# Attention with top-k and a channel mix: small products moved to GpSimd, weights split another way, weighings joined, mix chunks placed one by one

## The chip, the core and the metric

The kernel runs on one core of a Trainium2 chip. The metric is the device time of one execution in microseconds (us). Five engines work on their own queues, in the order of the program: TensorE (PE, with its weight loads shown apart as PEld), VectorE (DVE), ScalarE (ACT), GpSimd (POOL) and the queue that issues most transfers (SP).

## The reference

```python
scores = scale * q @ k.T                      # 8 batches, 8 heads, 576 x 576
kth = the 32nd largest score of each row
scores = where(scores >= kth, scores, -1e9)
attn = exp(scores - max); attn /= attn.sum(-1) + 1e-09
x = (attn @ v), heads side by side            # 8 x 576 x 512
xk = mu_k * x + (1 - mu_k) * x_prev           # x_prev: x one row earlier
xr = mu_r * x + (1 - mu_r) * x_prev
k = relu(xk @ w_k); v = (k * k) @ w_v         # 512 -> 1024 -> 512
out = sigmoid(xr @ w_r) * v
```

q, k and v are float32; w_k, w_v and w_r lie in memory as float64, 4 MB each for w_k and w_v and 2 MB for w_r.

## The kernel before, in words

**Attention.** Heads go in pairs; one pair of one batch has 1152 rows of scores, cut into 9 tiles of 128 rows, and the 288 tiles of the whole input come in 64 visits (tiles 0 to 3 of a pair, then 4 to 8). For a tile, TensorE makes the scores (`score`, `sliver`, or `score8` for the ninth tile, L824, L825, L833, L837), ScalarE copies them into `sc` (L842), and VectorE finds the 24 largest of a row: seven maxima of pieces (`cand`, L847), then three maxima with two removals between them (`best`, `drop`, L849, L852). `under` (L859) multiplies the largest and the 24th by two constants in one VectorE instruction of two columns; the results are the biases of `exps` and `count`. ScalarE's `count` (L867) marks what lies below the 24th, GpSimd's `below` (L869) multiplies scores and marks, VectorE takes the next eight (`eighth`, L870) and picks the threshold (`nine`, L872). ScalarE makes the exponentials (L875), VectorE masks and sums them (`mask`, L878), TensorE transposes them (`turn`, L883, and `turnl`, L892), ScalarE copies the transposes out, and TensorE multiplies by v (`weigh`, L912 and L913), one group of ten products for each two tiles. For up to four tiles the sums get 1e-9 (`inv`, L923) and a reciprocal (`inv2`, L924) on VectorE, are spread on GpSimd (L930), transposed (L934), copied out, and `place` (L947, L949) writes the rows of x into `xT`.

**Mix.** 18 chunks of 256 rows. GpSimd and ScalarE form xk and xr and split each into two parts in a reduced float32 (`change`, `share`, `add`, `xh`, `xl`); TensorE then multiplies in three products each (L620 to L622): 96 `hidden`, 24 `gate` and 48 `value` matmuls a chunk; ScalarE and GpSimd square and split what lies between (`relu`, `sq`, `r2`, `hl`), VectorE multiplies gate and value (`gated`, L1076).

**Weights.** 20 blocks of 128x512 float64 numbers are loaded as 32-bit words and turned into two float32 parts by bit work. Eight blocks of w_k go through four staging slots that later hold `hh` and `hl`; the twelve blocks of w_r and w_v go through two slots that lie in the `xT` buffer of the second batch, so `place` of that batch waits for the last of them. A block takes ScalarE `wabs` (L1118), VectorE `wclamp`, `wshift`, `wsign`, `wexp` (L1119 to L1122), ScalarE `wfine`, `whi` (L1126, L1127, for w_v `whalf` too), GpSimd `wmul` (L1128). The lower part is made for the first twelve blocks by three TensorE matmuls (`wsub`, L1134) and a ScalarE copy (L1136), for the last eight by a subtraction and an addition on GpSimd (L1138, L1139).

**What sets the order.** The program builds a graph of these steps and a planner lists them: each step has an engine, a cost, a latency and a key (its tile number plus an offset from the tables `OFF`, `HEAD`, `TAIL`), and of the steps of an engine that can start about first the one with the smallest key goes next. The mix is a single chain of pieces on TensorE, held back by `pace`, and the start of chunk c was worked out from the tiles that it needs (L997 to L999). The order of each queue is thus fixed before the run.

Of the kernel before, what the change touches and what calls it, by code (L numbers as in the profile page):

```python
# [20 lines left out]
TOPK = 32  # L21
# [24 lines left out]
BACK = False
HOLD = 0
PAIR = False
WCL = 0
# [4 lines left out]
def visits():  # L54

    vs = []
    for b in range(B):
        for k, part in enumerate(EDGE.get(b, HALVES)):
            for hp in range(HP)[::-1] if BACK and k % 2 else range(HP):
                if vs and vs[-1][:2] == (b, hp):  # L60
                    part = range(vs.pop()[2][0], part[-1] + 1)
                vs.append((b, hp, part))
                part = EDGE.get(b, HALVES)[k]
    return vs
# [1240 lines left out]
```

## Time and profile before

| what | value |
|---|---|
| median of 3 runs | 1198.69 us (1198.59 to 1199.99) |
| the profiled execution | 1199.56 us, its span 1197.8 us |
| granted TensorE clock, mean | 0.983 of full speed |
| instructions | 27941 |

The profile shows the span of one execution; what lies around it is 1.8 us here. In the rows below a busy share is the time in which an engine had an instruction at work, and a waiting time is put down to what ended it.

### The profile page before, as it was taken

Reading aid. Unit: us, or ns where it says so; the run is one execution under the profiler, and the core shown is the slowest. Engines: PE = TensorE matmul, PEld = TensorE weight load, DVE = VectorE, ACT = ScalarE, POOL = GpSimd, SP = SyncE. Lnnn points to the kernel's source line nnn. Section 1 sums busy time; section 2 is a strip of 40 time slices with the busy share of each in tenths; the row PEclk is TensorE's granted clock in tenths of the full one; section 3 lists DMA queues with packets and bytes.
Section 4 is the critical chain, followed back from the end, with each engine's and each line's share of the span. In section 5 each row is a group of like instructions: output and inputs, shape, how many; then the busy total and the mean of one; then the engine's idle time right before and its main releaser. Section 6 shows DMA issues by size and latency. Waiting matters only on the chain.

```text
span 1197.8 us, 27941 instructions
## 1 busy us (share of the span) xinstructions
PE 1145.7 (96%) x8717; PEld 877.5 (73%) x8717; DVE 1100.1 (92%) x6180; ACT 1030.9 (86%) x2205; POOL 865.8 (72%) x796
## 2 busy tenths in 40 slices
PE   5887799999999999999999999999999999999998
PEld 2444576878787877777777878787878787878886
DVE  6999999999999999999999999999999999999500
ACT  5898898999899999999899899989888989888631
POOL 2557896868686877778687677868686867777763
PEclk9887899999999999999999999999999999999999
DMA  6132212212122112221221212121221121211000
GB/s 241 50 130 86 83 46 76 63 55 69 53 79 67 54 54 76 63 81 43 77 64 54 69 54 69 54 72 54 67 68 58 56 68 56 68 48 37 18 19 21
DMA packets 36012, 78.43 MB, mean 65 GB/s; under 512 B 4112, under 2 KB 12304, under 8 KB 35856
## 3 DMA queue, kind: packets, MB, share of 16 engines
q1 hardware_dynamic: 35568, 76.17, 20.2%
q8 instruction: 71, 1.16, 0.4%
q14 instruction: 85, 0.70, 0.2%
q10 hardware_dynamic: 288, 0.39, 0.1%
HBM read 67.11 MB, written 9.44 MB: 64 GB/s over the span
## 4 chain that ended last, share of the span: by engine, by line
PE 48%; DVE 42%; ACT 6%; issue 2%; DMA 1%; POOL 0%; SPq 0%; DVEq 0%; ACTq 0%
DVE cand L847 11%; PE rot L620 8%; PE rot L622 8%; PE rot L621 8%; DVE E L878 8%; DVE top L870 7%; PE ps L912 6%; PE rot L883 6%; PE ps L837 5%; DVE top L849 4%; DVE cand L852 4%; DVE nine L872 2%; PE ps L824 1%; PE ps L913 1%; ACT sc L842 1%
## 5 line engine op out<-in xcount | busy, mean ns | idle before, releaser
L869 POOL TENSOR_TENSOR sg<-sc,sg 128x576 f32<-128x576 f32 x288 | 410.1, 1425 | 220.4 <-ACT sg L867 218.8
L847 DVE MAX8 cand<-sc 128x8 f32<-128x82 f32 (+1 forms) x2016 | 387.8, 231 | 5.5 <-ACT sc L842 4.6
L867 ACT ACTIVATE sg<-sc,seen 128x576 f32<-128x576 f32 x288 | 223.6, 777 | 24.8 <-DVE seen L859 23.6
L878 DVE SCALAR_TENSOR_TENSOR E<-sc,seen,se 128x576 f32<-128x576 f32 x288 | 230.4, 800 | 0.4 <-ACT se L875 0.2
L875 ACT ACTIVATE se<-sc,seen 128x576 f32<-128x576 f32 x288 | 215.5, 748 | 17.6 <-DVE E L878 12.4
L842 ACT ACTIVATE sc<-ps 128x576 f32<-128x576 f32 x288 | 184.9, 650 | 42.5 <-PE ps L837 15.6
L870 DVE MAX8 top<-sg 128x8 f32<-128x576 f32 x288 | 215.0, 747 | 4.1 <-POOL sg L869 3.9
L883 PE MATMUL rot<-ident,E 128*128 128x128 f32 x1152 | 179.7, 280 | 10.1 <-ACT ri L939 2.6
L883 PEld LDWEIGHTS rot<-ident,E 128*128 128x128 f32 x1152 | 131.5, 142 | 71.9 <-issue 11.1
L849 DVE MAX8 top<-cand 128x8 f32<-128x56 f32 x864 | 176.7, 207 | 1.6
L885 ACT ACTIVATE et<-rot 128x512 f32<-128x512 f32 x288 | 171.5, 598 | 3.7 <-PE rot L883 2.6
L620 PE MATMUL rot<-xh,wk 128*128 128x256 f32 x576 | 171.8, 298 | 0.3 <-ACT ri L940 0.2
L912 PE MATMUL ps<-et,v 128*64 128x128 f32 (+1 forms) x2560 | 166.8, 272 | 3.7 <-DVE xT L947 1.7
L912 PEld LDWEIGHTS ps<-et,v 128*64 128x64 f32 x2560 | 130.2, 139 | 53.3 <-issue 17.2
L621 PE MATMUL rot<-xl,wk 128*128 128x256 f32 x576 | 161.9, 281 | 0.5 <-POOL xl L1033 0.5
L622 PE MATMUL rot<-xh,wk 128*128 128x256 f32 x576 | 162.0, 281 | 0.0
L837 PE MATMUL ps<-K,qs 64*128 64x512 f32 x512 | 151.9, 671 | 0.0
L620 PE MATMUL rot<-wv,hh 128*128 128x512 f32 x288 | 123.7, 430 | 0.6 <-DVE eb L1076 0.6
L620 PEld LDWEIGHTS rot<-xh,wk 128*128 128x128 f32 x576 | 109.4, 190 | 9.0 <-issue 5.7
L852 DVE MATCH_REPLACE8 cand<-top,cand 128x56 f32<-128x56 f32 x576 | 115.5, 200 | 0.2 <-issue 0.2
L622 PE MATMUL rot<-wv,hl 128*128 128x512 f32 x288 | 113.7, 395 | 0.0
L621 PE MATMUL rot<-wv,hh 128*128 128x512 f32 x288 | 113.6, 394 | 0.0
(95 smaller groups left out, 2361.0 us busy)
## 6 DMA issues: line engine op xcount, KB each, us to landing
v<-in_v SPq DMA_DIRECT2D x64, 384.0 KB, 3.1
K<-in_k SPq DMA_DIRECT2D x64, 320.0 KB, 3.0
out<-eb SPq DMA_DIRECT2D x35, 256.0 KB, 2.0
qs<-in_q SPq DMA_DIRECT2D x32, 192.0 KB, 2.4
stage<-in_moe_w_k SPq DMA_DIRECT2D x8, 512.0 KB, 5.1
xT<-in_moe_w_v SPq DMA_DIRECT2D x8, 512.0 KB, 3.6
qs<-in_q SPq DMA_DIRECT2D x31, 128.0 KB, 2.1
xT<-in_moe_w_r SPq DMA_DIRECT2D x4, 512.0 KB, 6.1
```

Source lines behind the costliest of these rows:

```text
L620: return [nc.tensor.matmul(ps, lhsT=sh, rhs=mh, start=first, stop=False), nc.tensor.matmul(ps, lhsT=sh, rhs=ml, start=False, stop=False), ...
L621: nc.tensor.matmul(ps, lhsT=sh, rhs=ml, start=False, stop=False),
L622: nc.tensor.matmul(ps, lhsT=sl, rhs=mh, start=False, stop=last)]
L847: lambda T=T, c=c: nc.vector.max(T.cand.t[:, 8 * c:8 * c + 8], T.sc.t[:, CUTS[c]:CUTS[c + 1]]), reads=[T.sc], writes=[(T.cand, c)])
L849: plan.op(DVE, "best", n + BESTS * r, 120, 217, lambda T=T, r=r: nc.vector.max(T.top.t[:, r * 8:(r + 1) * 8], T.cand.t), reads=[T.cand], w ...
L867: lambda T=T, sn=sn: nc.scalar.activation(T.side.t, T.sc.t, AF.Sign, bias=sn(T, 1), scale=-BELOW, accum_out=T.top.t[:, TOPK:TOPK + 1]),
L869: plan.op(POOL, "below", n, 1375, 1430, lambda T=T: nc.gpsimd.tensor_mul(T.side.t, T.sc.t, T.side.t), reads=[T.sc], writes=[T.side])
L870: plan.op(DVE, "eighth", n, 660, 754, lambda T=T: nc.vector.max(T.top.t[:, 24:32], T.side.t), reads=[T.side], writes=[(T.top, 3)])
L875: plan.op(ACT, "exps", n, 667, 754, lambda T=T, pe=pe, sn=sn: nc.scalar.activation(pe.t, T.sc.t, AF.Exp, bias=sn(T, 0), scale=SCALE), read ...
L878: lambda T=T, U=U, pe=pe, sn=sn: nc.vector.scalar_tensor_tensor(T.e(), T.sc.t, sn(T, 2), pe.t, op0=OP.is_ge, op1=OP.mult, accum_out=U.rs.t ...
L883: return [nc.tensor.transpose(pt.t[:, c * 128:(c + 1) * 128], E.t[:, o + c * 128:o + (c + 1) * 128], ident) for c in range(NKC)]
L912: return [*[nc.tensor.matmul(pa[hs[j]], lhsT=vs[j][:, c, :], rhs=ms[c][j], start=(c == 0), stop=False) for c in range(NKC) for j in range(2)],
```

## The change

- `under` goes from VectorE to GpSimd, with its two constants in an SBUF tile `factors` instead of PSUM; `inv` too.
- The weight blocks are split another way. A block is loaded twice, the second time one 16-bit word further on (`wm`). ScalarE takes a scaled copy of the high words into PSUM (`wabs`) and their signs (`wsign`), VectorE shifts (`wshift`) and masks (`wrest`) with one side in PSUM, GpSimd multiplies in the sign (`wput`) and the exponent (`wmul`). `wclamp`, `wsub` on TensorE and the subtraction and addition on GpSimd are gone.
- The two weighings of a unit of four tiles are one step on TensorE, listed once both have their inputs.
- `score8` has one product with the last 64 keys instead of two; the tile of K is 704 columns wide instead of 640.
- The start of each mix chunk is a number of its own (`AT`); all tables of offsets have other numbers, there is a third table for the first 24 tiles (`FIRST`), and buffers differ: `et` 5 (was 3), `el` 3 (2), `sg` 3 (2), `eb` 3 (4), `K` 2 (3), no `lb`.

```diff
-MORE = dict(xh=2, xl=2, et=3, top=3, el=2, K=3, eb=4, lb=2)
+MORE = dict(xh=2, xl=2, et=5, top=3, el=3, eb=3, sg=3, K=2)
...
+AT = [-6.03, -8.616, 62.223, 51.725, 69.632, 81.783, 97.48, 87.342, 134.245, 89.408, 140.491, 139.103, 174.089, 182.425, 241.323, 261.83, 194.143, 348.355]
...
                         return [nc.tensor.matmul(ps[0].t, lhsT=qd, rhs=P.K.t[:, :MAIN], start=True, stop=True),
-                                *[nc.tensor.matmul(sl.t[:, MAIN:S], lhsT=qd, rhs=P.K.t[:, MAIN + h * REST:MAIN + (h + 1) * REST], start=h == 0, stop=h == 1) for h in range(2)]]
+                                nc.tensor.matmul(sl.t[:, MAIN:S], lhsT=qd, rhs=P.K.t[:, MAIN:S], start=True, stop=True)]
...
-                    plan.op(DVE, "under", n, 62, 160, lambda T=T, hp=hp: nc.vector.tensor_mul(T.seen.t[:, hp, 0:2, T.i], T.top.t[:, 0:24:23], X.ranks.t[:, 9:11]),
+                plan.op(POOL, "under", n, 140, 200, lambda T=T, hp=hp: nc.gpsimd.tensor_mul(T.seen.t[:, hp, 0:2, T.i], T.top.t[:, 0:24:23], factors),
...
-                    if not PAIR or u == (U.w - 1) // 2:
+                    if u == (U.w - 1) // 2:
                         fs, cs, rs, ws = zip(*U.weigh)
-                        U.weigh = []
                         plan.op(PE_, "weigh", n, sum(cs), sum(cs) + 197, lambda fs=fs: [x for f in fs for x in f()], reads=[x for r in rs for x in r] + [P.v], writes=ws, mode="W")
...
-                    plan.op(DVE, "inv", n, 60, 155, lambda w=w, U=U, pr=pr: nc.vector.tensor_scalar(pr.t[:, :w], U.rs.t[:, :w], 1e-9, None, op0=OP.add), reads=[U.rs], writes=[pr])
+                    plan.op(POOL, "inv", n, 120, 180, lambda w=w, U=U: nc.gpsimd.tensor_scalar(U.rs.t[:, :w], U.rs.t[:, :w], 1e-9, 1.0, op0=OP.add, op1=OP.mult), writes=[U.rs], mode="TS")
...
-            r = max(ready[b, u] for b, s, m in pieces for u in units_of(b, s, m)) + min(LAG, LAG0 + c * LAG1)
-            at = max(at, r)
-            key = lambda x, at=at, n=n: at + x * STEP * n / CH / 20
+            key = lambda x, at=AT[c], n=n: at + x * STEP * n / CH / 20
...
-            plan.op(DVE, "wclamp", key, 588, 692, lambda: nc.vector.tensor_scalar(pm.t, pm.t, ZERO, None, op0=OP.max), writes=[pm])
-            plan.op(DVE, "wshift", key, 588, 692, lambda: nc.vector.tensor_scalar(U(pm), U(pm), 3, 0x3FFFFFFF, op0=OP.logical_shift_left, op1=OP.bitwise_and), writes=[pm])
-        plan.op(DVE, "wsign", key, 588, 692, lambda: nc.vector.scalar_tensor_tensor(U(val), high(), 0xC0000000, U(pm), op0=OP.bitwise_and, op1=OP.bitwise_or), reads=[st, pm], writes=[val])
...
-            X.subs.append(plan.op(PE_, "wsub", key, 2050, 2250, rest, reads=[val, fine, (W, ('h', which))], writes=[pl], mode="T"))
-            done.append(plan.op(ACT, "wlo", key, 520, 630, lambda: nc.scalar.activation(lo, pl.t, AF.Copy), reads=[pl], writes=[(W, which)]))
...
+        plan.op(SP, "w", key, 600, 4500, lambda: nc.sync.dma_start(st.t.bitcast(U16), words), writes=[st])
+        plan.op(ACT, "wabs", key, 552, 640, lambda: nc.scalar.activation(pm.t, high().bitcast(F32), AF.Copy, scale=TINIER), reads=[st], writes=[pm])
+        plan.op(DVE, "wshift", key, 595, 695, lambda: nc.vector.tensor_scalar(bits(), pm.t.bitcast(U32), 3, 0x7FFFF000, op0=OP.logical_shift_left, op1=OP.bitwise_and), reads=[pm], writes=[val])
+        plan.op(ACT, "wsign", key, 552, 640, lambda: nc.scalar.activation(flat(), high().bitcast(F32), AF.Sign), reads=[st], writes=[mag])
...
+            plan.op(POOL, "wput", key, 1400, 1440, lambda: nc.gpsimd.tensor_mul(hi, val.t, flat()), reads=[val, mag], writes=[(W, ('h', which))])
+            plan.op(DVE, "wexp", key, 650, 750, lambda: nc.vector.tensor_scalar(flat().bitcast(U32), hi.bitcast(U32), 0xFF800000, None, op0=OP.bitwise_and), reads=[(W, ('h', which))], writes=[mag])
+        plan.op(SP, "wm", key, 600, 4500, lambda: nc.sync.dma_start(sm.t.bitcast(U16)[:, :2046], words[:, 1:2047]), writes=[sm])
+        plan.op(DVE, "wrest", key, 595, 695, lambda: nc.vector.tensor_scalar(pr.t.bitcast(U32), sm.t.rearrange("p (c t) -> p c t", t=2)[:, :, 0], 0x1FFFFFF, None, op0=OP.bitwise_and), reads=[sm], writes=[pr])
+        plan.op(ACT, "wfine", key, 560, 667, lambda: nc.scalar.activation(fine(), pr.t.bitcast(U32), AF.Copy, scale=2.0 ** (-37 if name == "v" else -36)), reads=[pr], writes=[sm])
+        done.append(plan.op(POOL, "wmul", key, 1400, 1440, lambda: nc.gpsimd.tensor_mul(lo, fine(), flat()), reads=[mag, sm], writes=[(W, which)]))
```

The order of the queues, at three places. First TensorE in the first third of the program, at the weighing of two tiles of one unit (et: transposed tiles, el: their last columns, ps: scores and sums, K and qs: the operands of a score). Before:

```order
L912 MATMUL ps<-et_112,v_84 64x128
L913 MATMUL ps<-el_115,v_84 64x128 x2
L837 MATMUL ps<-K_87,qs_88 128x512 x2
L620 MATMUL rot_143<-xh_121,wk_66 128x256
L621 MATMUL rot_143<-xl_123,wk_66 128x256
```

and in the changed program:

```order
L912 MATMUL ps<-et_114,v_87 64x128
L912 MATMUL ps<-et_115,v_87 64x128
L913 MATMUL ps<-el_120,v_87 64x128 x2
L912 MATMUL ps<-et_116,v_87 64x128
L912 MATMUL ps<-et_117,v_87 64x128
```

Before, a weighing of two tiles is followed by other work; now the weighing of the next two tiles stands directly behind it. Over the program the groups of weighings go from 160 to 96, the places where TensorE leaves a score or a weighing of half the array for something else from 288 to 224, and those where it enters one from whole-array work from 195 to 178.

Second, VectorE at the first weight blocks (stage and xT: staged words, rot: PSUM, eb, r: block-sized buffers). Before:

```order
L1119 TENSOR_SCALAR rot_141<-rot_141 128x512
L849 MAX top_96<-cand_94 128x8
L1119 TENSOR_SCALAR rot_142<-rot_142 128x512
L852 MATCH_REPLACE cand_94<-top_96,cand_94 128x56
L1120 TENSOR_SCALAR rot_141<-rot_141 128x512
L1120 TENSOR_SCALAR rot_142<-rot_142 128x512
L849 MAX top_96<-cand_94 128x8
L1121 SCALAR_TENSOR_TENSOR eb_127<-stage,rot_141 128x512
L859 TENSOR_TENSOR seen_103<-top_96,se 128x2
L1121 SCALAR_TENSOR_TENSOR eb_128<-stage,rot_142 128x512
```

and in the changed program:

```order
L1120 TENSOR_SCALAR rot_143<-xT_137 128x512
L858 MATCH_REPLACE cand_96<-top_98,cand_96 128x56
L1110 TENSOR_SCALAR eb_133<-rot_142 128x512
L855 MAX top_98<-cand_96 128x8
L1120 TENSOR_SCALAR rot_142<-stage 128x512
L858 MATCH_REPLACE cand_96<-top_98,cand_96 128x56
L1110 TENSOR_SCALAR eb_134<-rot_144 128x512
L855 MAX top_98<-cand_96 128x8
L1110 TENSOR_SCALAR eb_135<-rot_143 128x512
L1120 TENSOR_SCALAR rot_144<-stage 128x512
L1118 TENSOR_SCALAR r_131<-wr_70 128x512
```

A block has three VectorE instructions instead of four, and the product `seen<-top` has left the queue. In the old order all 80 weight instructions of VectorE stand ahead of the 28th mask; in the new one 54 of 60 stand ahead of the 30th, and the last ahead of the 37th. The first hidden product of the mix stands on TensorE behind 19 turned tiles before and behind 20 now.

Third, GpSimd in the middle of the program (sg: marked scores, hl, xl, xm: parts of the mix, seen: the two products). Before:

```order
L869 TENSOR_TENSOR sg_99<-sc_90,sg_99 128x576
L1033 TENSOR_TENSOR xl_123<-xm_120,xh_121 128x512
L1033 TENSOR_TENSOR xl_123<-xm_119,xh_121 128x512
L869 TENSOR_TENSOR sg_100<-sc_91,sg_100 128x576
L930 TENSOR_SCALAR ri_116<-rs_108 128x128
```

and in the changed program:

```order
L1026 TENSOR_TENSOR xl_129<-xm_126,xh_127 128x512
L1026 TENSOR_TENSOR xl_129<-xm_125,xh_127 128x512
L864 TENSOR_TENSOR seen_106<-top_100,factors 128x2
L869 TENSOR_TENSOR sg_102<-sc_92,sg_102 128x576
L1045 TENSOR_TENSOR r_132<-r_132 128x512
L864 TENSOR_TENSOR seen_106<-top_98,factors 128x2
L869 TENSOR_TENSOR sg_103<-sc_93,sg_103 128x576
```

The small product of a tile now stands in the queue of GpSimd's long products, about one tile ahead of the `below` of its own tile.

## Rows read from the trace of the kernel before

**Rows 1.** The page's first part: busy us, share of the span, instructions.

```profile
PE 1145.7 (96%) x8717; PEld 877.5 (73%) x8717; DVE 1100.1 (92%) x6180; ACT 1030.9 (86%) x2205; POOL 865.8 (72%) x796
```

**Rows 2.** Stretches: length, busy us of PE, PEld, DVE, ACT, POOL, clock, DMA share, GB/s.

```profile
8.20:160.00 151.80, 115.06 (x653) 70.09 (x654) 147.19 (x677) 128.95 (x262) 99.13 (x83) 0.88 0.32 105
160.00:1120.00 960.00, 955.98 (x7617) 744.57 (x7618) 944.74 (x5482) 874.81 (x1893) 725.42 (x670) 1.00 0.20 61
1120.00:1190.00 70.00, 70.00 (x439) 60.67 (x436) 6.83 (x18) 25.13 (x50) 40.40 (x36) 1.00 0.06 20
```

**Rows 3.** One stretch, TensorE alone.

```profile
160.00:1190.00 1030.00, 1025.98 (x8052) 1.00 0.19 58
```

**Rows 4.** One line of each: operation, count, ns min/median/max, first and last start.

```profile
L1119 DVE TENSOR_SCALAR rot<-rot x20: 669/683/699, 10.6 to 152.4; 128x512 f32<-128x512 f32 x20
L859 DVE TENSOR_TENSOR seen<-top,se x288: 130/143/163, 14.7 to 1118.1; 128x2 f32<-128x2 f32 x144
L620 PE MATMUL rot<-xh,wk x576: 277/281/581, 116.9 to 1174.6; 128*128 128x256 f32 x192
```

**Rows 5.** Timeline of VectorE, 12.8 to 14.8 us: start, us, line.

```profile
12.81 1.28 DVE L1120 TENSOR_SCALAR rot<-rot 128x512 uint32<-128x512 uint32 x2
...
14.72 0.15 DVE L859 TENSOR_TENSOR seen<-top,se 128x2 f32<-128x2 f32 x1
14.78 0.68 DVE L1121 SCALAR_TENSOR_TENSOR eb<-stage,rot 128x512 uint32<-128x512 uint32 x1
```

**Rows 6.** Stretches, the instructions of L859 alone.

```profile
0.00:160.00 160.00, 4.21 (x29) 0.88 0.34 113
```

**Rows 7.** Timeline of TensorE, 805 to 814 us.

```profile
805.63 0.60 PE L883 MATMUL rot<-ident,E 128*128 128x128 f32 x4
806.16 1.09 PE L912 MATMUL ps<-et,v 128*64 128x128 f32 x16
807.08 0.39 PE L913 MATMUL ps<-el,v 128*64 128x128 f32 x4
807.40 1.13 PE L837 MATMUL ps<-K,qs 64*128 64x512 f32 x4
...
812.11 0.60 PE L883 MATMUL rot<-ident,E 128*128 128x128 f32 x4
812.54 1.02 PE L824 MATMUL ps<-K,qs 128*128 128x512 f32 x2
813.40 0.56 PE L825 MATMUL ps<-K,qs 128*128 128x64 f32 x4
813.80 0.28 PE L892 MATMUL ps<-ident,E 128*128 128x128 f32 x1
```

**Rows 8.** Groups of GpSimd instructions by form: busy us, mean ns, idle before.

```profile
L1128 POOL TENSOR_TENSOR lb<-lb,r 128x512 f32<-128x512 f32 x20 | 25.7, 1285 | 12.4 <-ACT lb L1126 9.9 <-DVE r L1122 2.5
L1029 POOL TENSOR_TENSOR xm<-xm,xT 128x256 f32<-128x256 f32 x16 | 10.7, 690 | 1.1 <-ACT xm L1024 1.0
L1029 POOL TENSOR_TENSOR xm<-xm,xT 128x128 f32<-128x128 f32 x16 | 7.1, 446 | 0.2 <-ACT xm L1024 0.2
```

**Rows 9.** Waits of GpSimd: who waited for whom, us, times, longest.

```profile
POOL sg L869 <- ACT sg L867: 218.8, 154, 15.0
```

**Rows 10.** Loads of weight blocks: KB each, median us to landing.

```profile
xT<-in_moe_w_v SPq DMA_DIRECT2D x8, 512.0 KB, 3.6
xT<-in_moe_w_r SPq DMA_DIRECT2D x4, 512.0 KB, 6.1
```

**Rows 11.** Stretches, TensorE's `wsub` (L1134) alone: busy PE, busy PEld.

```profile
0.00:160.00 160.00, 28.43 (x60) 11.38 (x60) 0.88 0.34 113
```

**Rows 12.** Stretches of all engines, columns as in rows 2.

```profile
0.00:20.00 20.00, 10.48 (x21) 4.15 (x22) 10.55 (x41) 9.54 (x16) 4.44 (x12) 1.00 0.89 334
...
130.00:140.00 10.00, 6.09 (x37) 3.61 (x36) 9.00 (x32) 7.26 (x14) 9.27 (x9) 0.66 0.15 43
140.00:150.00 10.00, 9.41 (x78) 7.54 (x77) 9.07 (x50) 8.27 (x20) 7.57 (x7) 1.00 0.18 68
```

More of the change, by code (lines that the diff above doesn't have):

```diff
@@ L57, in visits @@
     for b in range(B):
[L58 to L61, printed above, removed]
+        for part in EDGE.get(b, HALVES):
+            for hp in range(HP):
                 vs.append((b, hp, part))
-                part = EDGE.get(b, HALVES)[k]
     return vs
@@ L89 @@
-TAIL = dict(addr=9.764, wshift=-54.034, wexp=12.766, sq=46.852, lowt=0.774, sliver=-0.915, whi=18.971, xlk=10.89, xhk=11.972, store=21.562,
-            nine=-22.73, best=11.307, wclamp=-30.249, lowr=15.632, hl=-29.505, turni=-0.007, xhr=-12.539, relu=-3.644, kt=-26.88, drop=1.635,
-            gate=23.895, score8=-15.705, eighth=4.543, under=5.446, inv2=-16.489, v=18.41, w=-5.629, wmul=11.119, wfine=-13.156, lowest=23.573,
-            gexp=-39.54, score=-0.308, sharek=16.794, wabs=-18.436, exps=3.896, nmu=-26.956, below=0.218, changek=-0.251, lowc=14.381, wsub=8.41,
-            inv=-21.671, low=9.578, gated=-2.041, turnl=3.662, place=0.456, ri=-33.859, r2=4.155, weigh=1.655, spread=-7.304, kq=12.986, cand=16.257,
-            value=25.102, hidden=7.542, zero=-6.282, ranks=-14.357, mu=-14.658, count=20.929, mask=-6.883, wsign=1.775, xlr=17.098, wlo=-3.664,
-            keep=-1.091, addk=2.852, el=-2.717, sharer=-17.211, turn=1.382, et=4.439, whalf=5.878)
+NEAR = dict(PE=142.316, ACT=94.901, DVE=1.447, POOL=234.747, SP=6.125)
@@ new lines @@
+HEAD = dict(sharek=-47.371, zero=154.778, lowt=-23.559, score8=-11.785, store=209.645, el=-79.186, gate=-26.338, turni=91.426, sq=26.461, hl=113.15,
+            relu=-47.049, wmul=-27.583, low=-6.219, xhk=61.499, inv=110.857, v=-12.116, gated=-131.363, xlk=16.829, turn=42.663, r2=4.269,
+            xlr=16.635, addr=-200.707, ri=-66.902, below=-14.314, best=-24.605, wabs=-59.334, lowr=180.774, sliver=-116.326, nmu=14.466, kq=141.279,
+            changek=39.743, count=-13.892, hidden=6.777, addk=-98.359, xhr=95.257, lowc=60.575, eighth=-56.451, w=172.797, kt=1.172, wshift=-10.774,
+            wexp=15.565, ranks=119.206, spread=32.638, mask=-44.708, whi=179.551, drop=-62.419, gexp=65.164, keep=-94.404, inv2=-20.263, mu=-116.499,
+            weigh=-64.727, turnl=48.3, score=-5.275, under=-90.964, nine=-79.706, place=-5.27, sharer=50.724, et=33.131, wfine=30.879,
+            wsign=-118.488, exps=-49.391, lowest=-68.808, value=60.46, cand=6.626, wrest=5.672, wm=2.948, wput=-29.083)
@@ new lines @@
+TAIL = dict(addr=75.077, wshift=-71.426, wexp=88.368, sq=220.928, lowt=-151.351, sliver=-126.01, whi=-14.333, xlk=100.276, xhk=54.542, store=-72.657,
+            nine=53.016, best=55.339, lowr=9.427, hl=81.731, turni=-109.29, xhr=45.326, relu=-18.048, kt=30.108, drop=85.184, gate=-36.159,
+            score8=-63.376, eighth=-43.894, under=-43.046, inv2=-36.699, v=29.142, w=-96.933, wmul=0.662, wfine=26.729, lowest=-64.048, gexp=123.791,
+            score=-32.419, sharek=-17.199, wabs=-168.587, exps=2.264, nmu=-196.418, below=26.843, changek=-82.372, lowc=17.854, inv=270.105,
+            low=-26.01, gated=77.754, turnl=33.065, place=59.611, ri=124.319, r2=-54.949, weigh=-98.505, spread=-120.091, kq=-22.273, cand=60.211,
+            value=5.334, hidden=-50.412, zero=35.483, ranks=-27.964, mu=85.532, count=39.835, mask=101.415, wsign=37.272, xlr=118.137, keep=-40.713,
+            addk=3.005, el=-27.772, sharer=-104.183, turn=-6.619, et=-42.42, wrest=30.561, wm=-111.8, wput=-71.442)
@@ L776, in attend @@
         buf = plan.buf
[L777 to L778 removed]
+        xT = {}
+        seen = None
         for p, (b, hp, part) in enumerate(visits):
```

184 lines of the change are left out of this document (76 added, 108 removed).

## The prediction

> **What bounds the kernel now.** I read the busy times first, then cut the span into stretches, then asked which engine never rests in each. Over the span TensorE is busy 96% and VectorE 92% [rows 1], which names no single bound. The stretches do [rows 2]. From 8.2 to 160 us VectorE is busy 147.2 of 151.8 us, while TensorE has 36.7 us without work: this is the **head**, in which the weights are converted beside the first 29 tiles. From 160 to 1190 us TensorE is busy 1026 of 1030 us [rows 3]: there nothing but TensorE's own work sets the time. VectorE is nearly full too until 1120 us [rows 2], but it is done 70 us before TensorE, so it follows there. The end is therefore the length of the head plus the TensorE work that is left behind it. GpSimd, with 725 of 960 us in the long stretch, has 235 us of room.
>
> **The head.** VectorE decides, so I count what leaves and joins its queue up to the 29th tile. Before, all 80 weight instructions lie there; after, 54 of 60 do, the rest behind: 26 fewer. One takes 0.684 us by its record [rows 4], but two in a row take 1.28 us together, so the next starts after 0.59 us [rows 5]. 26 x 0.59 = 15.3 us (by records, 17.8). That the new shift reads PSUM and writes SBUF, and the new mask the other way round, has no row; both lie between forms with one or two PSUM sides that take 0.67 to 0.69 us [rows 4, 5], so I take them as equal. The 29 `under` products have 4.2 us of records there [rows 6]; the next instruction starts 0.06 us behind one [rows 5], so they give back 1.7 to 4.2 us, taken as 2. `inv`, nine times here, is as small: below 1 us, taken as 0.5. Against it stands one tile more ahead of the first hidden product (20 instead of 19): VectorE's share of a tile here is (147.2 - 80 x 0.59)/29 = 3.4 us, but the tile's TensorE work is then done too, so between 0 and 3.4 us, taken as 2. Sum: 15.3 + 2 + 0.5 - 2 = 15.8 us, of which I grant **15 us**; bounds 10 and 20.
>
> What covers the rest of the head. TensorE loses `wsub`, 28.4 us of its time [rows 11]; it waits there anyway, so nothing for the sum by itself. ScalarE loses 32 passes over a block (two copies and the halving) and gains 20 signs: a little lighter at 129 of 151.8 us [rows 2]. GpSimd changes 20 products and 16 sums for 40 products of 1.285 us [rows 8], +5 us on 99 of 151.8. Loads: 20 more of about 512 KB, 10.5 MB over some 145 us, +72 GB/s on 105 [rows 2], where the first 20 us carried 334 [rows 12]. The twelve blocks of w_r and w_v now send two loads each through the same two slots, the second copy being held from its issue until `wmul`: at least 6.1 us of landing [rows 10] plus mask, copy and product (0.68 + about 0.65 + 1.29), near 9 us. Twelve of those fit in the 165 us until the 38th tile if each takes under 13 us. If this cover goes, the value products of chunk 0 wait, 12 us for each us that a hold is longer. The wider K tile (352 instead of 320 KB) and one K slot fewer are hidden: a visit of four or five tiles passes between two loads.
>
> **The long stretch.** Only what shortens TensorE counts; VectorE's lighter queue (259 `under`, 87 `inv`) gives nothing where TensorE is full.
> - `score8`: four records of the 64 columns run from 813.40 to 813.80 us [rows 7]; two go, so 0.20 us x 32 = 6.4 us.
> - Joined weighings: sixteen records of a weighing take 0.92 us, so four take 0.23, but the last four take 0.32 until the next start: 0.09 us for leaving [rows 7]. Four transposes take 0.53 us ahead of a weighing and 0.43 ahead of whole-array work: 0.10 for entering [rows 7]. Leavings fall by 64, enterings by 17: 64 x 0.09 + 17 x 0.10 = 7.5 us. Bounds: 0, if the cost stays at the seam inside a joined pair, and 64 x 0.19 = 12.2 if each pair saved both.
> - A tenth (29 of 288 tiles) of both lies in the head and counts nothing: 0.9 x 13.9 = **12.5 us**.
>
> **The moves on GpSimd.** A product of 128x2 has no row there. The nearest are 0.690 us at 256 columns and 0.446 at 128 [rows 8]; carried down the same line to 2 columns it is 0.21 us. Bounds: 0.14, its time on VectorE [rows 4], and 0.446. 288 of them and 96 `inv` of the same size add 80 us, giving 866 + 5 + 80 = 951 us (at the upper bound 1042), below the new span: hidden by GpSimd's room in the long stretch. `count` on ScalarE now waits for a queue in which a product of 1.4 us may stand ahead; what is queued behind is that tile's `below`, `eighth` and `mask`. The order issues `under` a tile ahead of its `below`, and `sg`, `et` and `el` have more buffers, so I price this at 0; the rival below prices it if that is wrong.
>
> **Sum.** Against the profiled execution: 1199.6 - 15 - 12.5 = **1172 us**. That execution is 0.9 us above the median of the runs, less than what the terms are uncertain by.
>
> **Rivals.**
> 1. *The head keeps its length.* Without `wsub` TensorE is idle more often there, and its clock already falls where it rests: 0.66 of full in the ten us in which it was busy 6.1, 1.00 in the next with 9.4 busy [rows 12], a mixture of 1.2 and 2.4 GHz. If scores and transposes at 1.2 GHz come too late for VectorE, its relief turns into waiting: 1199.6 - 12.5 = 1187 us. Against it: at half rate all through, the head's TensorE work without `wsub`, 115.1 - 28.4 = 86.7 us at a clock of 0.88 [rows 2, 11], would be 86.7 x 0.88/0.5 = 153 us, just over the 145 that I forecast; but the clock would have to stay at 1.2 GHz throughout, and even the ten us with 6.1 busy had 0.66. So it is close enough for 0.17. The Trainium skill, TensorE: Matmul & The Clock Gate (section "What's actually happening"), says that the throttled state is the default and activity releases it; by it the clock of the head falls further. The rows agree in direction.
> 2. *The seam costs as before*, so that joining does not do what it promises: only `score8` counts, 0.9 x 6.4 = 5.8, giving 1179 us. For it: the 0.09 us may belong to the last four products themselves. Chance 0.12.
> 3. *Slower: GpSimd becomes the bound of the long stretch.* Its work from 160 to 1120 us rises from 725 [rows 2] by 259/288 of 80 to 797 us. Of its idle time, 219 us in the whole span end at ScalarE's `count` [rows 9]. The new span leaves 960 - 12.5 - 797 = 150 us of idle time where there were 235; if the waits stay, the stretch is 85 - 12.5 = 72 us longer and the kernel ends at 1199.6 - 15 + 72 = 1257 us. It decides once idle time there stays above 150 us, 0.58 us a tile. Half of that excess would give about 1215 us. Against it: a wait of an engine with nothing else to do is slack and shrinks by itself. The Trainium skill, GPSIMD Engine Reference (section "Engine selection"), tells to keep elementwise products on VectorE, as GpSimd takes about twice as long for two inputs. The rows agree, with 0.21 against 0.14 us. Chance 0.10.
> 4. Rivals 1 and 2 together: 1194 us, chance 0.06.
>
> **How the numbers follow.** The forecast has 0.51, rivals 1 to 4 have 0.17, 0.12, 0.10 and 0.06, and 0.04 is left for a head shorter by 20 us and all of the upper bound of joining (1162 us or less). The range takes in the forecast with its bounds (head 10 to 20, joining 0 to 12.2), and rivals 1 and 2: 1160 to 1190 us, with 0.80. What a measurement can tell from no change is 0.2%, 2.4 us: faster means below 1196.3. Faster: 0.51 + 0.17 + 0.12 + 0.04 and most of rival 4 is 0.87; the same 0.04, from rival 4 and a weak rival 3; slower 0.09, from rival 3.
>
> **What would show it.** Right: the first hidden product (116.9 us before [rows 4]) starts at 104 to 109 us, VectorE stays over 95% busy until then, TensorE is full from about 145 us, two records instead of four stand behind `score8`, and the seam of two weighings has no 0.09 us. Rival 1 shows VectorE waiting for ScalarE's copies or TensorE in the head. Rival 3 shows TensorE idle behind 160 us, ending at VectorE or ScalarE steps that wait for GpSimd, and GpSimd over 95% busy or waiting in turn. The forecast is wrong if TensorE has more than some 15 us of idle time behind the head.

## The result, and the profile after

The changed kernel takes 1169.62 us (median of 4 runs, 1167.78 to 1171.0) against 1199.31 for the kernel before in the same session: ratio 0.9752, 95% interval 0.9735 to 0.9768. The profiled execution took 1169.5 us, where the forecast was 1172. The total is right. Its two terms are not, as the rest shows: the head gave less than was claimed, the long stretch more, and by all signs for a reason that the prediction had priced at nothing.

The page of the changed kernel, its first part (to be held against [rows 1]):

```profile
PE 1096.4 (94%) x8593; PEld 860.0 (74%) x8593; DVE 1068.1 (91%) x5773; ACT 1015.9 (87%) x2193; POOL 934.2 (80%) x1185
```

To see where the time went, the two kernels must be compared at equal states of the program, not at equal times. A good mark is the mask on VectorE (L878 in both kernels, one a tile). Here are the stretches that end at masks 32, 128 and 288 (the last), counting L878 alone: length, busy us, instructions (a mask and the reading of its sum). Before:

```profile
0.00:174.70 174.70, 25.07 (x63) 0.89 0.32 106
174.70:522.80 348.10, 77.66 (x193) 1.00 0.21 66
522.80:1122.50 599.70, 129.28 (x321) 1.00 0.19 59
```

and after:

```profile
0.00:162.50 162.50, 25.10 (x63) 0.86 0.51 169
162.50:510.60 348.10, 77.73 (x193) 1.00 0.23 72
510.60:1095.80 585.20, 129.46 (x321) 1.00 0.21 63
```

The mix products stand alike at these marks. In the same stretches the first product of each triple (L620 before, L630 after) counts, before:

```profile
0.00:174.70 174.70, 13.64 (x40) 7.99 (x40) 0.89 0.32 106
174.70:522.80 348.10, 104.98 (x292) 55.25 (x292) 1.00 0.21 66
522.80:1122.50 599.70, 195.65 (x550) 104.29 (x550) 1.00 0.19 59
```

and after 40, 292 and 554. So the same program state is reached 12.2 us sooner at mask 32, still 12.2 sooner at mask 128, and 26.7 sooner at mask 288, with four triples more done. With marks at 48 and 64 as well, all counted in VectorE's timeline, and the start of the last TensorE instruction:

| mask | before, us | after, us | gain so far |
|---|---|---|---|
| 16 | 100.6 | 96.9 | 3.7 |
| 32 | 174.6 | 162.4 | 12.2 |
| 48 | 233.5 | 225.7 | 7.8 |
| 64 | 290.8 | 283.5 | 7.3 |
| 128 | 522.7 | 510.5 | 12.2 |
| 288 | 1122.4 | 1095.7 | 26.7 |
| end | 1191.5 | 1162.1 | 29.4 |

(At mask 64 the changed kernel has 12 mix products fewer behind it, at mask 128 the same 996.) **The head** gains 12.2 us by the 32nd tile and gives 4.4 back by the 48th; 21.6 of the 29.4 us come behind that. VectorE alone, up to the 48th mask, before and after:

```profile
0.00:233.50 233.50, 221.24 (x1117) 0.92 0.30 99
```

```profile
0.00:225.70 225.70, 208.96 (x1021) 0.89 0.45 147
```

It has 12.3 us less to do, and waits 16.7 us instead of 12.3: that makes the 7.8 us.

One profile is not exact to 1 us here. In that of experiment 1, the same kernel once more, every mark from the 16th on lies 2.0 to 2.3 us later (99.2, 164.7, 285.8, 1097.7 us), all of it lost ahead of the 16th, while the stretch from mask 64 to mask 288 has the same length (811.9 and 812.2 us).

The stretch from mask 64 to mask 288, all engines, columns as in [rows 2]. Before:

```profile
290.90:1122.50 831.60, 828.76 (x6610) 646.16 (x6609) 815.11 (x4712) 755.35 (x1635) 623.34 (x574) 1.00 0.20 60
```

After:

```profile
283.60:1095.80 812.20, 809.90 (x6564) 641.99 (x6563) 795.30 (x4416) 749.03 (x1639) 674.70 (x875) 1.00 0.21 65
```

It is 19.4 us shorter. TensorE is busy 99.7% of it in both kernels and VectorE 98.0% and 97.9%, and both have some 19 us less to do: 18.9 and 19.8. From this view alone it can't be told which of the two gave the time. GpSimd took its new work without trouble: its small products, at 0.195 us in the median, cost about what was estimated (0.21 us),

```profile
L864 POOL TENSOR_TENSOR seen<-top,factors x288: 182/195/382, 15.9 to 1091.4; 128x2 f32<-128x2 f32 x144
```

and the waits of its long product for ScalarE's `count`, 218.8 us before [rows 9], are fewer:

```profile
POOL sg L869 <- ACT sg L867: 85.7, 97, 2.2
```

The joined weighings look as forecast. TensorE's timeline after, 604.89 to 606.30 us (the first row ends the first weighing of a pair):

```profile
604.89 0.39 PE L913 MATMUL ps<-el,v 128*64 128x128 f32 x4
605.11 1.04 PE L912 MATMUL ps<-et,v 128*64 128x128 f32 x16
605.98 0.39 PE L913 MATMUL ps<-el,v 128*64 128x128 f32 x4
606.30 0.66 PE L883 MATMUL rot<-ident,E 128*128 128x128 f32 x4
```

From start to start, four short products take 0.22 us up to the weighing that follows and 0.32 up to a transpose; the sixteen long ones take 0.87 us instead of 0.92 [rows 7]. Over the whole run the weighings take 176.2 us in this way, 187.8 before.

### The profile page after: what moved, and what is told of

It reads as the page before. It is cut to its first block, busy times and chain, and to the rows that moved or that the text cites. A ratio compares the mean times of both kernels' runs of the same rounds, so it can differ in the third digit from the quotient of the medians.

```text
span 1167.7 us, 27723 instructions
## 1 busy us (share of the span) xinstructions
PE 1096.4 (94%) x8593; PEld 860.0 (74%) x8593; DVE 1068.1 (91%) x5773; ACT 1015.9 (87%) x2193; POOL 934.2 (80%) x1185
## 5 line engine op out<-in xcount | busy, mean ns | idle before, releaser
L853 DVE MAX8 cand<-sc 128x8 f32<-128x82 f32 (+1 forms) x2016 | 375.2, 230 | 6.3 <-ACT sc L848 5.1
L875 ACT ACTIVATE se<-sc,seen 128x576 f32<-128x576 f32 x288 | 216.5, 752 | 19.4 <-DVE E L878 18.5
L878 DVE SCALAR_TENSOR_TENSOR E<-sc,seen,se 128x576 f32<-128x576 f32 x288 | 230.7, 801 | 0.3
L883 PE MATMUL rot<-ident,E 128*128 128x128 f32 x1152 | 183.1, 285 | 40.5 <-DVE E L878 21.7
L630 PE MATMUL rot<-xh,wk 128*128 128x256 f32 x576 | 169.6, 294 | 0.0
L912 PE MATMUL ps<-et,v 128*64 128x128 f32 (+1 forms) x2560 | 161.5, 269 | 1.8 <-ACT el L894 1.3
L632 PE MATMUL rot<-xh,wk 128*128 128x256 f32 x576 | 160.8, 279 | 0.0
L843 PE MATMUL ps<-K,qs 64*128 64x512 f32 x512 | 154.9, 684 | 0.2
L912 PEld LDWEIGHTS ps<-et,v 128*64 128x64 f32 x2560 | 132.8, 139 | 25.0 <-issue 8.5
L630 PE MATMUL rot<-wv,hh 128*128 128x512 f32 x288 | 121.3, 421 | 0.0
L630 PEld LDWEIGHTS rot<-xh,wk 128*128 128x128 f32 x576 | 109.6, 190 | 6.4 <-issue 4.5
L631 PE MATMUL rot<-wv,hh 128*128 128x512 f32 x288 | 112.6, 391 | 0.0
```

What stands on the lines that cost most here:

```text
L630: return [nc.tensor.matmul(ps, lhsT=sh, rhs=mh, start=first, stop=False), nc.tensor.matmul(ps, lhsT=sh, rhs=ml, start=False, stop=False), ...
L631: nc.tensor.matmul(ps, lhsT=sh, rhs=ml, start=False, stop=False),
L632: nc.tensor.matmul(ps, lhsT=sl, rhs=mh, start=False, stop=last)]
L853: lambda T=T, c=c: nc.vector.max(T.cand.t[:, 8 * c:8 * c + 8], T.sc.t[:, CUTS[c]:CUTS[c + 1]]), reads=[T.sc], writes=[(T.cand, c)])
L875: plan.op(ACT, "exps", n, 667, 754, lambda T=T, pe=pe, sn=sn: nc.scalar.activation(pe.t, T.sc.t, AF.Exp, bias=sn(T, 0), scale=SCALE), read ...
L878: lambda T=T, U=U, pe=pe, sn=sn: nc.vector.scalar_tensor_tensor(T.e(), T.sc.t, sn(T, 2), pe.t, op0=OP.is_ge, op1=OP.mult, accum_out=U.rs.t ...
```

## The experiments

All of them change one thing in the one kernel or the other, with what it drags along. Where the order of the planner is kept, every engine's instructions stay where they are, except for those named. The kernel before, timed beside each group of experiments, took 1199.2 to 1199.7 us (medians), so that times of different groups can be held against each other.

**1. The changed kernel again**, on another chip, as a measure.

> The changed kernel once more, as the measure for the three that follow on this chip. 1168 to 1171 us, ratio 0.974 to 0.977 to the kernel before. Of the spacing inside a run of mix products (0.2329 us from start to start of a 512-column product in the profile before, 0.2300 in the profile after; 0.1182 and 0.1155 for the 256-column one): if it belongs to the kernel it is 0.230 and 0.1155 here again; if it differs from execution to execution, it may be either.

1171.26 us, ratio 0.9765 (0.9751 to 0.9778). The spacing is 0.230 and 0.1158 us again: it belongs to the kernel. Experiments 8 to 10 follow it up.

**2. and 3. The ninth tile's short product**, in two halves again in the changed kernel, in one piece in the kernel before.

```diff
-  nc.tensor.matmul(sl.t[:, MAIN:S], lhsT=qd, rhs=P.K.t[:, MAIN:S], start=True, stop=True)]
+  *[nc.tensor.matmul(sl.t[:, MAIN:S], lhsT=qd, rhs=P.K.t[:, S + h * REST:S + (h + 1) * REST],
+                     start=h == 0, stop=h == 1) for h in range(2)]]
```

> The changed kernel, with the short product of the ninth tile made in two halves again, in the same order and with the same plan. If TensorE bounds the stretch: in the profile 0.39 us from the start of the short products to the next instruction (0.17 in the changed kernel), 32 x 0.22 = 7 us, so 6 to 7 us slower than the changed kernel, 1176. If TensorE has room there (rival): within 1 us of it.

> The kernel before, with the ninth tile's short product in one piece (and the array of K 64 columns wider for it, 352 KB a transfer instead of 320), nothing else, same plan. If it is worth what its records say, wherever it stands: 32 x 0.22 = 7 us, of which those in the first 160 us (TensorE not full there) give nothing, so 5.5 to 7 us faster than the kernel before, 1192 to 1194, ratio 0.994 to 0.9955. Rival (the longer transfers of K, or a wait that takes its place): within 1 us of it.

Halved again: 1172.67 us, ratio 0.9788 (0.9774 to 0.9801), 1.4 us above experiment 1 by the medians and 2.8 by the ratios. In one piece: 1197.13 us, ratio 0.9984 (0.9975 to 0.9993), 2.1 us. The records are as priced. In the timeline of the changed kernel, and then of experiment 2:

```profile
815.76 0.33 PE L831 MATMUL ps<-K,qs 128*128 128x64 f32 x2
815.92 0.39 PE L933 MATMUL rot<-ident,ri 128*128 128x128 f32 x2
```

```profile
629.45 0.55 PE L831 MATMUL ps<-K,qs 128*128 128x64 f32 x4
629.84 0.28 PE L892 MATMUL ps<-ident,E 128*128 128x128 f32 x1
```

0.16 to 0.17 us to the next start against 0.39, some 7 us over 32 tiles. But only a third of it or a little more is seen in the time, in both directions. From mask 64 to mask 288 experiment 2 takes 814.7 us, 2.8 more than experiment 1, and experiment 3 has

```profile
290.40:1120.10 829.70, 826.10 (x6559) 640.55 (x6555) 814.33 (x4713) 755.64 (x1636) 623.54 (x574) 1.00 0.20 62
```

1.9 us less than the kernel before, where 5.5 us of TensorE's starts are gone. The rest turns up as a little longer spacing of other TensorE instructions and as idle time, beside a VectorE that is busy as long as before. A TensorE that is busy 99.7% by its records is not one whose every us counts.

**4. The joined weighings taken apart**, in the changed kernel with its order: the second of a pair is moved behind the next transpose or run of mix products, or the one ahead of the pair is moved between the two.

> The changed kernel, with the 64 joined pairs of weighings taken apart by one TensorE instruction or run (a transpose or a run of mix products) moved between the two; everything else in the same order on every engine. Theory of the leaving cost: 64 x (0.10 for leaving + 0.05 for entering again) = 9.6 us of TensorE, and up to 64 x 0.09 more where a run of mix products is cut; 7 to 13 us slower than the changed kernel, 1177 to 1183. Rival (the seam costs the same inside a pair): within 1 us of it.

1202.86 us, ratio 1.0029 (1.002 to 1.0039): 31.6 us slower than experiment 1, far above both theories. From mask 64 to 288:

```profile
290.60:1129.30 838.70, 827.12 (x6563) 641.28 (x6564) 799.53 (x4416) 750.89 (x1639) 675.47 (x875) 1.00 0.20 63
```

VectorE now rests for 39 of 839 us. In the waits of that stretch there is one of 25.6 us that has no place among the larger ones of the changed kernel:

```profile
ACT sc L894 <- PE ps L959: 25.6, 25, 1.9
```

The copy of the scores (`keep`) waits for the last product of the weighing that was moved back: the scores' last columns and the sums of the weighings lie in one bank of PSUM. So the experiment moved a weighing into other work's way, and its time says nothing on what the seam is worth. The seam's own cost is back about as expected: behind 160 us the weighings take 167.6 us from start to start (waits left out) instead of 158.0.

**5. and 6. Joined weighings alone, in the kernel before**, first with its order kept and the first weighing of a pair moved down to the second, then with an order that its planner lays out anew.

```diff
-PAIR = False
+PAIR = True
-MORE = dict(xh=2, xl=2, et=3, top=3, el=2, K=3, eb=4, lb=2)
+MORE = dict(xh=2, xl=2, et=5, top=3, el=2, K=3, eb=4, lb=2)
```

> The kernel before, with 60 of the 64 pairs of weighings joined: the first is moved down to stand right ahead of the second, all else in its order on every engine (two more buffers for et, a third for el). TensorE saves 60 x (0.10 + 0.05) = 9 us of switching in its records, and more where two runs of mix products become one. If TensorE alone bounds the stretch: 8 to 10 us faster than the kernel before, 1189 to 1191. If VectorE bounds it as well (theory A): a third of it, as with the ninth tile's product, 2 to 4 us faster, 1195 to 1197. Rival 2 (the seam costs as before): within 1 us.

> The kernel before, with joined weighings alone, its planner laying out the order anew with them (five buffers for et instead of three), nothing else. TensorE saves 64 x 0.15 = 10 us of switching. If TensorE alone bounds the stretch: 8 to 10 us faster than the kernel before, 1189 to 1191. Theory A: 2 to 5 us faster, since VectorE's work for a tile stays as it is, 1194 to 1197. Rival 2: within 1 us.

With the order kept: 1238.17 us, ratio 1.032 (1.0306 to 1.0334). In this run the third buffer for `el` lies on an array in which weights are still being split, so that some of the weights are spoilt; that adds no instruction behind the head, and still the stretch from mask 64 to 288 is 31 us longer than before. Which waits make that up was not followed. With a new order: 1205.31 us, ratio 1.0051 (1.0037 to 1.0064), 5.6 us slower, though the weighings take 10.6 us less from start to start. The row of experiment 6 for that stretch:

```profile
290.90:1126.60 835.70, 825.66 (x6612) 649.59 (x6611) 817.48 (x4716) 754.89 (x1639) 624.37 (x577) 1.00 0.19 61
```

TensorE has 3 us less to do than before and idles 7 us more; VectorE has 2 us more to do and waits a little longer. So the kernel before gets no time from joining in either order: 10 us of TensorE's switching go, and waits take more than that. (The tables by which this planner orders were made for single weighings, so the 5.6 us are what joining loses at most, not its price; in the changed kernel, whose tables were made for pairs, its worth was not measured.)

**7. and 7b. The bias products back on VectorE**, in the changed kernel with its order, first with the factors in SBUF, at the places that the products have in that order (and the 1e-9 additions with them), then with the factors in PSUM as before, each right behind the search that it reads. The edit of 7b, shortened:

```diff
-plan.op(POOL, "under", n, 140, 200, lambda T=T, hp=hp: nc.gpsimd.tensor_mul(T.seen.t[:, hp, 0:2, T.i],
-        T.top.t[:, 0:24:23], factors), ...
+plan.op(DVE, "under", n, 140, 200, lambda T=T, hp=hp: nc.vector.tensor_mul(T.seen.t[:, hp, 0:2, T.i],
+        T.top.t[:, 0:24:23], X.ranks.t[:, 9:11]), ...
```

> The changed kernel, with the 288 bias products and the 1e-9 additions back on VectorE, at the same places of the order. In the stretch of tiles VectorE is busy 98.3% in both profiles (idle 14.2 of 797 us and 13.4 of 793), and these instructions took 0.069 + 0.022 us a tile there before. Theory A (VectorE is a bound of that stretch beside TensorE): most of 288 x 0.091 = 26 us comes back, 15 to 26 us slower than the changed kernel, 1186 to 1197. Theory of the prediction (TensorE alone bounds it, the move is worth 2.5 us in the head): 0 to 5 us slower. Rival 3 (GpSimd's extra instructions cost): faster.

> The changed kernel, with the 288 bias products back on VectorE with the factors in PSUM, as the kernel before has them, each right behind the last search that it reads; the 1e-9 additions stay on GpSimd, and everything else keeps its place. VectorE gets 288 x 0.069 = 20 us more (the price of such a product in the stretch of tiles before). Theory A (VectorE bounds that stretch beside TensorE, and the GpSimd product held up the one in SBUF): 12 to 20 us slower than the changed kernel, 1183 to 1191. Theory of the prediction (TensorE alone bounds the stretch): 0 to 3 us slower, for the head. Rival 3 (GpSimd's 288 products cost): faster.

With factors in SBUF 1287.77 us, ratio 1.0733 (1.0718 to 1.0748): 117 us slower than experiment 1. With factors in PSUM 1229.46 us, ratio 1.0249 (1.0235 to 1.0263): 58 us. VectorE's group in the first and in the second (minimum, median and maximum in ns):

```profile
L888 DVE TENSOR_TENSOR seen<-top,factors x288: 128/206/1273, 17.0 to 1211.0; 128x2 f32<-128x2 f32 x144
```

```profile
L892 DVE TENSOR_TENSOR seen<-top,se x288: 157/158/161, 15.5 to 1152.5; 128x2 f32<-128x2 f32 x144
```

In the first the product of two columns takes up to 1.27 us; the last section tells why. The second is free of that, but has a wait of its own: its product, placed right behind the search, waits 30.7 us in all (1.7 in the kernel before), half of it for ScalarE's exponentials,

```profile
L892 DVE TENSOR_TENSOR seen<-top,se 128x2 f32<-128x2 f32 x288 | 45.6, 158 | 30.7 <-ACT se L903 15.0 <-ACT sc L876 0.9
```

since these are written into the same array of PSUM. So 58 us is too much for the move and only says on which side the truth lies: 20 us more on VectorE's queue are not hidden under a TensorE that is "full". "0 to 3 us" falls.

What the two runs show beyond that stands in the stretch from mask 64 to mask 288, for experiment 1, 7 and 7b in turn:

```profile
285.90:1097.80 811.90, 809.75 (x6564) 642.06 (x6564) 795.27 (x4416) 748.62 (x1639) 673.89 (x875) 1.00 0.20 65
```

```profile
309.70:1214.80 905.10, 843.29 (x6566) 644.35 (x6565) 890.50 (x4714) 760.37 (x1639) 624.47 (x576) 0.99 0.18 58
```

```profile
296.40:1156.60 860.20, 832.75 (x6565) 641.46 (x6566) 827.19 (x4640) 757.97 (x1639) 640.36 (x651) 1.00 0.19 61
```

In experiment 7 VectorE is busy 95.2 us longer and the stretch is 93.2 us longer; in 7b it is busy 31.9 us longer, waits 16.4 us longer, and the stretch is 48.3 us longer. What VectorE gets there, the stretch takes. And TensorE, with the same instructions in all three, is "busy" for 33.5 and 23.0 us more: its busy time holds waits that its records do not show as idle.

**8. to 10. Addresses.** The changed kernel allocates one small array more ahead of the others (`factors`, 8 bytes, for which 32 are reserved), and so everything behind it lies 32 bytes further on. An unused array of 32 bytes does the same to the kernel before, and the opposite to the changed one.

```diff
     flag = consts.tile([1, 1], I32, name="flag")
+    pad = consts.tile([128, 8], F32, name="pad")
+    nc.gpsimd.memset(pad, 0.0)
```

> The kernel before, with an unused array of 32 bytes a partition ahead of the others, so that the addresses of xh, xl, hh, hl, E, et and el move from 32 beyond a multiple of 64 to a multiple of 64 (as they lie in the changed kernel), and those of K, qs and v the other way. Theory (the spacing of mix products hangs on that): 0.230 and 0.1155 us in a run where the profile before has 0.2329 and 0.1182, 3024 x 2.8 ns = 8 us of TensorE, and 3 to 8 us faster than the kernel before, 1191 to 1196. Rival (it hangs on something else of the change): 0.2329 stays, within 1 us.

> The changed kernel, with the same unused 32 bytes: xh, xl, hh, hl, E, et and el at 32 beyond a multiple of 64, as they lay before. Theory: spacing 0.2329 and 0.1182 again, 3 to 8 us slower than the changed kernel, 1174 to 1179. Rival: 0.230 and 0.1155 stay, within 1 us of it.

> The changed kernel, with two unused arrays of 32 bytes a partition, so that K, qs and v begin at a multiple of 64 as well as xh, xl, hh, hl, E, et and el. If the spacing of weighings and scores hangs on it as that of mix products does: up to 2560 x 2.8 ns = 7 us of TensorE less, 1 to 4 us faster than the changed kernel, 1167 to 1170, and faster than both. Rival (only what mix products read matters): within 1 us of it.

| kernel | 512-column product, us | 256-column, us | time, us | ratio (95%) |
|---|---|---|---|---|
| before | 0.2329 | 0.1181 | 1199.2 to 1199.7 | 1 |
| before, shifted | 0.2308 | 0.1159 | 1196.01 | 0.9972 (0.9962 to 0.9983) |
| after (exp. 1) | 0.2300 | 0.1158 | 1171.26 | 0.9765 (0.9751 to 0.9778) |
| after, shifted | 0.2326 | 0.1182 | 1174.30 | 0.9789 (0.9776 to 0.9802) |
| after, both parts at multiples of 64 | 0.2330 | 0.1192 | 1177.70 | 0.9815 (0.9802 to 0.9829) |

The spacing is the mean inside runs, for the value and the hidden products, from 200 to 1000 us. It is seen best at the end of the program, where TensorE is all but alone: the last value has 48 products, of which these are the first and the last. Before, before shifted, after, after shifted:

```profile
1180.56 0.40 PE L620 MATMUL rot<-wv,hh 128*128 128x512 f32 x1
...
1191.53 0.39 PE L622 MATMUL rot<-wv,hl 128*128 128x512 f32 x1
```

```profile
1176.01 0.39 PE L622 MATMUL rot<-wv,hh 128*128 128x512 f32 x1
...
1186.67 0.39 PE L624 MATMUL rot<-wv,hl 128*128 128x512 f32 x1
```

```profile
1151.43 0.39 PE L630 MATMUL rot<-wv,hh 128*128 128x512 f32 x1
...
1162.08 0.39 PE L632 MATMUL rot<-wv,hl 128*128 128x512 f32 x1
```

```profile
1156.15 0.39 PE L632 MATMUL rot<-wv,hh 128*128 128x512 f32 x1
...
1167.12 0.40 PE L634 MATMUL rot<-wv,hl 128*128 128x512 f32 x1
```

10.97, 10.66, 10.65 and 10.97 us: 32 bytes more or less decide over 2.9% of a run of products. Over all 3024 products that is 6.3 us of TensorE in the kernel before, of which 3 to 4 us are seen in its time. So some 3 us of the change's 29.7 come from where its new array put the others. The theory that multiples of 64 are what counts falls with experiment 10, where all of xh, xl, hh and hl lie at such multiples, as in the changed kernel, but 64 bytes further on: the hidden and value products are slow again (the 512-column products of the gate, at 0.2305 us, are not), and the kernel is 6 us slower than experiment 1.

**11. The head.** The shift of the weights' words made twice over, in the changed kernel with its order.

```diff
-lambda: nc.vector.tensor_scalar(bits(), pm.t.bitcast(U32), 3, 0x7FFFF000, ...)
+lambda: [nc.vector.tensor_scalar(bits(), pm.t.bitcast(U32), 3, 0x7FFFF000, ...) for _ in range(2)]
```

> The changed kernel, with the shift of the weights' words on VectorE made twice over, 20 more VectorE instructions on weights (80 in all, as the kernel before has), in the same order. Theory (the head is bound by VectorE): 20 x 0.4 to 0.6 = 8 to 12 us slower than the changed kernel, 1179 to 1183, the first gate as much later than 154. Rival 1 (TensorE's slow clock and idle time keep the head's length): within 2 us.

1180.82 us, ratio 0.9847 (0.9834 to 0.9861), 9.6 us slower than experiment 1. The 32nd mask is at 173.6 us instead of 164.7, 8.9 us later, the last one also 8.9 and the end 8.9. Masks alone, first experiment 11, then experiment 1:

```profile
0.00:173.70 173.70, 25.11 (x63) 0.86 0.47 158
```

```profile
0.00:164.80 164.80, 25.15 (x63) 0.82 0.49 166
```

Up to the 32nd mask 19 of the 20 extra shifts have run, VectorE has 12.8 us more to do, and waits 3.9 us less than in experiment 1: the 8.9 us are what is left. So most of what VectorE gets in the head is paid, not all, and nothing of it is caught up later. Rival 1, within 2 us, falls.

## Why the prediction was right in the sum and wrong in its parts

**That VectorE decides over the head: right.** Experiment 11 shows it, at a clock of TensorE that fell as rival 1 had it. From 50 to 110 us the changed kernel has

```profile
50.00:80.00 30.00, 16.82 (x88) 9.77 (x88) 28.23 (x137) 25.38 (x51) 22.75 (x26) 0.73 0.64 218
80.00:110.00 30.00, 19.84 (x137) 13.65 (x137) 28.71 (x135) 25.03 (x53) 21.30 (x26) 0.72 0.41 133
```

a granted clock of 0.73 and 0.72, a mixture of the levels 1.2 and 2.4 GHz, with TensorE busy for 16.8 and 19.8 of 30 us. VectorE waited for 3.1 of these 60 us, 0.4 in the kernel before. None of these waits ends at TensorE, and 0.7 us of them at a copy of ScalarE's: that is all that came of rival 1. That low activity and a low clock go together is what the Trainium skill says (TensorE: Matmul & The Clock Gate, section "What's actually happening"); the trace agrees in direction.

**"15 us" for the head: wrong by half, in two places.** First, of the 26 weight instructions by which VectorE is lighter up to the 29th tile, 20 are gone and 6 are only later. The prediction wrote "54 of 60 do, the rest behind" and gave that rest no price. It is there: L1115, a step of w_v on VectorE, starts for the last time at 182.6 us, and takes 1.02 us a piece in the median,

```profile
L1115 DVE TENSOR_SCALAR r<-eb x8: 409/1018/1472, 67.4 to 182.6; 128x512 uint32<-128x512 uint32 x8
```

and the 16 tiles up to the 48th take 63.3 us instead of 58.9: 4.4 us back, half of it more work and half of it more waits of VectorE, with TensorE busy 35.3 of 40 us from 160 to 200 us. That leaves 12.2 - 4.4 = 7.8 us.

The other place is VectorE's waits, for which the prediction had no term. It shows at the sign that was named, the first hidden product at "104 to 109 us". It started at 115.9, 1 us sooner than before. All 26 instructions had been counted ahead of it, but by then only 15 fewer had run (47 against 62), some 9 us. These went to the tile that the order has more in front of it, some 3 us, and to VectorE's waits up to there, 14.0 us instead of 10.2. In the kernel before it never waits for a load of weights; in the changed one, which loads every block twice, 3.3 us of its waits there end at the second loads (L1120 is the step that reads them), and 6.1 us in experiment 1:

```profile
DVE rot L1120 <- DMA stage<-in_moe_w_k: 3.8, 3, 1.9
DVE rot L1120 <- DMA xT<-in_moe_w_r: 1.5, 1, 1.5
DVE rot L1120 <- DMA xT<-in_moe_w_v: 0.8, 2, 0.4
```

**That from 160 us on "nothing but TensorE's own work sets the time": the step that failed.** It was read from TensorE's 1026 busy us of 1030 [rows 3], and VectorE's 945 of 960 were set aside because VectorE is done 70 us earlier. But in an order that is fixed, each mix piece has its place between tiles, and where VectorE is the later one TensorE's short waits hide in the spacing of its instructions: in experiments 7 and 7b the same instructions were busy for 33.5 and 23.0 us more. Taking 7 us from TensorE alone gave 2 (experiment 3), 6 gave 3 to 4 (experiment 8), and 10.6 gave none (experiment 6). So `score8`, forecast at 6.4 x 0.9 = 5.8 us, is worth 1.4 to 2.8, and joining, forecast at 6.7, showed no gain that stands by itself.

**"VectorE's lighter queue gives nothing where TensorE is full": wrong, and by the count the largest term.** Between masks 64 and 288 a bias product took VectorE 0.069 us from start to start in the kernel before, and the additions 0.022 us a tile. 224 x 0.091 = 20.4 us, and the stretch got 19.4 us shorter, with VectorE at 98% in both kernels. That TensorE lost as much at the same time (18.9 us: half product, seams, spacing, longer runs of mix products) is why both could move together; experiments 3, 6 and 8 say that TensorE's part alone would not have done it, and experiments 7 and 7b show that this stretch takes on what VectorE gets. How the 19.4 us divide between the two is not settled: putting VectorE's products back could not be done without a new wait, and no run took them alone out of the kernel before. Nor was the new order, with its tables and buffers, tried without the rest, so that a part of the 19.4 us may be its own; only the waits that the records show do not point to it, as VectorE's are 16.5 us in this stretch before and 16.9 after, TensorE's 2.8 and 2.3.

**That GpSimd hides 80 us more: right.** It had 934 us to do (951 forecast). A product of two columns took 0.195 us, 1.4 times the 0.143 on VectorE and not the "about twice" that the prediction cites. Rival 3 did not come: the time for which it waits for `count` fell instead of staying, as slack does. **The seam inside a pair** is gone, as forecast, and rival 2 is wrong on the records; that it would be worth 7.5 us was wrong for the reason above. **The loads** of the second copies of w_k and w_v land in 4.7 and 3.6 us in the median, no slower than the first ones (4.9 and 4.6), but VectorE waits for some of them, as said. TensorE idles 8 us from 160 to 1120 us, under the 15 that the forecast set as its limit.

So 15 + 12.5 = 27.5 was close to the 29.4 by luck, by two errors of opposite sign: 7 us too much for the head, 9 too little for what follows.

## What to carry to other kernels

Two engines at 98 and 99.7% are two bounds, not one and a follower: price a change on each of them, and take as its worth the time that both lose together; a saving on TensorE alone showed a third to a half of itself here, or none. A busy share near 100% can hold waits. Work that leaves a stretch for a later one is not saved: look what the later stretch is bound by. And before a difference of 0.3% is put down to an instruction, compare the spacing of instructions that the change does not touch: a new array of 8 bytes moved all others and was worth 3 us.

## What was not expected of the hardware

**A product of two columns that takes 1.27 us.** With both inputs in SBUF, VectorE's 128x2 product took 0.128 us at best and 1.273 us at worst (experiment 7); with one of them in PSUM 0.157 to 0.161 in all 288 cases (7b). One of the long ones, on VectorE and then on GpSimd at the same time:

```profile
501.31 1.24 DVE L888 TENSOR_TENSOR seen<-top,factors 128x2 f32<-128x2 f32 x1
```

```profile
499.98 2.55 POOL L1050 TENSOR_TENSOR xl<-xm,xh 128x512 fp32r<-128x512 f32 x2
```

It ends with the second of two GpSimd differences of 1.3 us. The Trainium skill (SBUF — State Buffer, section "Who interferes with whom") has the reason: a VectorE instruction with two SBUF inputs fetches the second through the read interface that it shares with GpSimd, and the shared pair of ports is an exclusive lock. The trace agrees. L1115 and L1118 of the changed kernel, one SBUF side to another, show a like thing: the 7 of the 20 that start while GpSimd has nothing at work take 0.41 to 0.42 us, and the 13 others, 0.63 to 1.47 us, all end 0.28 to 0.29 us behind a GpSimd instruction that was at work when they started. So the kernel before was right to keep these factors in PSUM, and the changed kernel may keep them in SBUF only because GpSimd reads them now.

**The spacing of matmuls hangs on where their operands lie in SBUF.** 0.2267 or 0.2333 us for a 512-column product at the end of the program, with one instruction each of VectorE and ScalarE beside them and the clock at 1.00, and, as means inside runs, 0.1158, 0.1182 or 0.1192 for a 256-column one, by 32 or 64 bytes of address. Which addresses are the good ones is open: multiples of 64 alone are not enough (experiment 10), and no run varied one operand by itself.
